# Retention in pairs of units ahead of two feed-forward layers

## The chip, the cores and the metric

The kernel runs on one core of a Trainium2 chip. The metric is the device time of one launch in microseconds (us), the median of three runs. TensorE is called PE here, VectorE DVE, ScalarE ACT, GpSimd POOL, and SyncE SP. SP only issues DMAs, in the order of its queue.

## The reference

The input is q, k and v for 4 batches, 8 heads, 576 positions and 64 features a head. Retention is attention without a softmax: the scores are weighted by a power of the distance, cut off above the diagonal, and multiplied with v. Two feed-forward layers of 2304 tokens, 512 features and 2048 hidden features follow.

```python
scores = scale * np.matmul(q, k.transpose(0, 1, 3, 2))
Dmat = np.where(rel >= 0, gamma[:, None, None] ** rel[None, :, :], 0.0)
attn = np.matmul(scores * Dmat[None], v)          # -> x [2304, 512]
h = x @ w_in;  x = (h * np.tanh(softplus(h))) @ w_out      # layer 1 (Mish)
h = x @ w2_in; out = (h * sigmoid(1.702 * h)) @ w2_out     # layer 2
```

All of it is in float32.

## The kernel before

Retention is cut into 20 units: per batch four chunks of 128 positions and a short one of 64 (`UNITS`, numbered 0 to 19; 4, 9, 14 and 19 are short, and 0, 5, 10 and 15 open a batch). One DMA of 1 MB brings a full unit into one of six buffers, a smaller one a short unit. The weighting is carried in the data: POOL scales v of a unit ahead of its use (`decay_v`, L870), and the last step scales the product (`gt`).

A unit has four groups of matmuls on PE. *Scores* (`sc`, L884) multiply k and q in 64-row halves of the array, 128 columns wide. *Carried* products (L940) multiply the state of the positions before with q, in 64 x 64 quarters. *Sums* (`ds`, L908) add k times v to the state, with 128 rows and 64 columns; ACT copies the sums to SBUF as the next `state` (`take`). *Masked* products (L952) multiply v with the masked scores `pm`, in the same shape as the sums. A unit that opens a batch has no carried group, a short unit has no sums. DVE makes `pm` out of the scores (L889) and `X` out of the finished products `o` (`finish`, L971). The scores of all units go round three PSUM banks, 7, 4 and 6.

`manual_schedule` keeps each engine's instructions as the code issues them. Up to unit 3 a unit is done after the other. From unit 4 on the scores of unit u + 1 stand ahead of the carried products, sums and masked products of unit u.

Layer 1 needs its weights as two float32r parts, a high one and a low one. `convert` makes them from 64-bit words, in steps that are dealt out over the units and, later, over the slots of layer 1: clamp (DVE), two copies to other words (ACT, `raw`), sign and shift (DVE), join (POOL, L220), high part (ACT, `w`), low part (L253, on POOL for the first two blocks of 128 hidden features, on DVE for the rest). `EARLY_AT` says at which unit the first two blocks are loaded and clamped; every later step waits for the next `position` call of its engine. A slot of layer 1 is one product `up` of a block of tokens with a block of weights (two slots per weight block: 512 tokens, then 256), one product `down` that belongs to three slots before, and `elementwise`: Mish and high part of `g` on ACT, low part of `g` on DVE (L460). Slots 0 and 1 stand between the last units: `up(0)` behind unit 17, `up(1)` behind unit 18, their `elementwise` behind the products of units 18 and 19. Slots 2 and on are in `first_layer`; slot 4 is the first that needs weight block 2.

Of the kernel before, what the change touches and what calls it, by code (L numbers as in the profile page):

```python
# [9 lines left out]
F32 = mybir.dt.float32  # L10
# [5 lines left out]
ALU = mybir.AluOpType  # L16
# [3 lines left out]
B, H, S, D = 4, 8, 576, 64  # L20
NT, DM, DFF = 2304, 512, 2048
P = 128
NPAIR = H // 2
NK = DM // P
# [77 lines left out]
def retention_mish_gelu_kernel(ctx: ExitStack, tc: tile.TileContext, qkv, w1, w2, first_unit, rests, out):  # L102
# [73 lines left out]
    def place(m):  # L176
        return keep if m in KEPT else late[0]
# [620 lines left out]

    def attention():
        with tc.tile_pool(name="att", bufs=1) as ap, tc.tile_pool(name="outs", bufs=1, space=PSUM) as outs:  # L800
            sc_banks = itertools.cycle((7, 4, 6))

            loaded = {}

# [46 lines left out]
            gt = ap.tile([P, NCH, NPAIR, P], F32, name="gt")  # L851
            load(0)
            unused = outs.tile([P, 2, NB], F32, tag="o1", name="unused")[:, 0, :P]
# [22 lines left out]

            def scores(u):
                n = CH[UNITS[u][1]][1]
                qt, kt = loaded[u][:2]
                sc = [quarters(psum(next(sc_banks), "sc")) for _ in range(2)]  # L880
                for p in range(NPAIR):
                    for j in range(2):
                        sl = slice(64 * j, 64 * j + 64)
                        nc.tensor.matmul(sc[j][rows(j, n), p, :n], lhsT=kt[sl, p, :], rhs=qt[sl, p, :], start=True, stop=True)  # L884
                pm[u] = []
                for j in range(2):
                    t = ap.tile([P, NPAIR, P], F32, tag="pm", name="pm", bufs=4)
                    at = rows(j, n)
                    nc.vector.tensor_tensor(  # L889
                        out=t[at, :, :n],  # L890
                        in0=sc[j][at, :, :n],
                        in1=cm[at, at].unsqueeze(1).to_broadcast([n, NPAIR, n]),
                        op=ALU.mult,
                    )
                    pm[u].append(t)

            def update(u):
# [23 lines left out]
                act(state[u % 2], sums[0][:, :, :D])  # L921
                return state[u % 2]

            def outputs(u, before, between=lambda: None):
                c = UNITS[u][1]
                n = CH[c][1]
                qt, _, v, _ = loaded[u]
                o = outs.tile([P, 2, NB], F32, tag=f"o{u % 2}", name="o")
                o = o[:, :, : 2 * P].rearrange("p r (c n) -> p r c n", c=2)

                def place(h):

                    j = h % 2
                    return o[64 * j : 64 * j + 64, h // 4, h // 2 % 2, :n]

                for p in (0, 2) if c else ():
                    for r in range(2):
                        for q in (p, p + 1):
                            sl = slice(64 * r, 64 * r + 64)
                            nc.tensor.matmul(  # L940
                                place(4 * r + q),
                                lhsT=before[sl, q, :],
                                rhs=qt[sl, q, :],
                                start=(p == 0),
                                stop=True,
                                skip_group_check=True,
                            )
                between()
                for h in range(H) if n == P else (0, 1, 4, 5, 2, 3, 6, 7):
                    r, p = divmod(h, NPAIR)  # L950
                    at, q = rows(r, n), h if n == P else p
                    nc.tensor.matmul(  # L952
                        place(h),
                        lhsT=v[at, q * D : (q + 1) * D],
                        rhs=pm[u][r][at, p, :n],
                        start=(c == 0 and p < 2),
                        stop=True,
                        skip_group_check=True,
                    )
                loaded.pop(u)  # L960
                return o

            def finish(u, o):
                b, c = UNITS[u]
                t0, n = CH[c]
                g0 = b * S + t0
                part = 0
                halves = lambda t: t.rearrange("p (r c) n -> p r c n", r=2)
                while part < n:
                    w = min(n - part, 2 * TH - (g0 + part) % (2 * TH))  # L970
                    nc.vector.tensor_tensor(  # L971
                        out=halves(cut(slice(None), g0 + part, w)),
                        in0=o[:, :, :, part : part + w],
                        in1=halves(gt[:, c, :, part : part + w]),
                        op=ALU.mult,
                    )
                    part += w

            decay_v(0)
            scores(0)  # L980
            act(gt[:, 0, :, : GROW[0]], first)
            for j, w in enumerate(GROW):
                for p in range(NPAIR):
                    act(gt[:, 0, p, w : 2 * w], gt[:, 0, p, :w], scale=grow[:, p, j : j + 1])
            for u in range(n_u):
                step = u - n_u
                if u - 1 in wide and wide.index(u - 1) + len(buffers) < len(wide):
                    n = wide[wide.index(u - 1) + len(buffers)]
                    load(n)
                    if n + 1 not in wide:  # L990
                        load(n + 1)
                if u + 1 < n_u:
                    decay_v(u + 1)
                position("pool", step)
                position("fetch", step)
                if u == 0:
                    for n in wide[NCH : len(buffers)]:
                        load(n)
                if NCH - 1 < u < n_u - 1:
                    scores(u + 1)  # L1000
                position("act early", step)
                x_jobs = [split_x((0, SIDE)[k // NK], k % NK) for k, at in enumerate(X_UNITS) if at == u]
                before = now[0]

                def step_state():
                    update(u)
                    now[0] = take(u)
                    if u == NCH - 1:
                        scores(u + 1)

                o = outputs(u, before, step_state)
                position("vector", step)
                for job in x_jobs:
                    job()
                if 0 < u < NCH - 1:
                    scores(u + 1)
                if u < NCH - 1:
                    n = CH[u + 1][1]
                    for p in range(NPAIR):
                        act(gt[:, u + 1, p, :n], gt[:, 0, p, :n], scale=steps[:, p, u + 1 : u + 2])  # L1020
                if u == n_u - 2:
                    elementwise(0, jobs=False)
                finish(u, o)
                if u == n_u - 1:
                    elementwise(1, jobs=False)
                if u == 0:
                    scores(1)
                position("act late", step)
                if u == n_u - 3:
                    up(0)  # L1030
                if u == n_u - 2:
                    up(1)

    first_ring = {}
    R_RING = [(tag, 2) for tag in ("w0a", "w0b", "x0", "x1")]
# [270 lines left out]
```

## Time and profile before

| | |
|---|---|
| median of 3 runs | 802.55 us (802.33 to 802.9) |
| profiled execution: time, span | 802.39 us, 800.7 us |
| PE busy | 795.6 us (99% of the span) |
| DVE, ACT, POOL busy | 564.0, 433.9, 200.6 us |
| retention on PE (first scores to `up(2)`) | 5.02 to 65.28 us |
| layer 1, first slot with weight block 2 | 72.40 us |

The span goes from the first to the last recorded instruction; the time lies 1.69 us above it. PE is busy from end to end, so a time is read best from the chain of waits, which gives the moments at which one group of matmuls follows another; a group that takes longer than its like has a wait in it. The other engines matter where one of their instructions is what PE waits for.

### The profile page before, as it was taken

To read this page: it belongs to the slowest core of one execution; us is meant where nothing else is said; L and a number is where in the kernel's file an instruction comes from. 1 tells how busy PE (TensorE), PEld (TensorE's weight loads), DVE (VectorE), ACT (ScalarE), POOL (GpSimd) and SP (SyncE) were. 2 spreads that over 40 slices of the span, in tenths; PEclk is the share of its full clock that TensorE was granted. 3 is DMA by queue.
4 is the path that set the end of the run, shared out by engine and by line. 5 is a ranking of instruction groups with operands and counts; after the bars stand their busy time and mean duration, and the time that the engine had idled before them with its cause. 6 is when DMAs were issued, how large, how long until landed. Compare 5 with 4: busy or idle time off the path is not lost.

```text
span 800.7 us, 14255 instructions
## 1 busy us (share of the span) xinstructions
PE 795.6 (99%) x5394; PEld 754.1 (94%) x5394; DVE 564.0 (70%) x980; ACT 433.9 (54%) x845; POOL 200.6 (25%) x262
## 2 busy tenths in 40 slices
PE   9999999999999999999999999999999999999998
PEld 8888888889999999999999999999999999999998
DVE  4788888877676766577667376898555887656775
ACT  4247676756665655666566464664233763234542
POOL 3684222210576640367560051000000000000000
PEclk9999999999999999999999999999999999999999
DMA  9985768845889995698996599888878888888884
GB/s 365 417 357 186 261 212 276 288 144 211 281 294 343 311 312 167 215 328 301 335 312 214 202 349 379 262 275 269 295 256 248 256 275 285 277 251 255 251 272 159
DMA packets 92325, 219.15 MB, mean 274 GB/s; under 512 B 6496, under 2 KB 52576, under 8 KB 90464
## 3 DMA queue, kind: packets, MB, share of 16 engines
q1 hardware_dynamic: 92112, 218.04, 80.8%
q8 instruction: 43, 0.70, 0.3%
q14 instruction: 26, 0.21, 0.1%
q10 hardware_dynamic: 144, 0.20, 0.1%
HBM read 169.45 MB, written 48.76 MB: 273 GB/s over the span
## 4 chain that ended last, share of the span: by engine, by line
PE 98%; DVE 1%; ACT 0%; issue 0%; DVEq 0%
PE p L734 22%; PE p L685 21%; PE acc L1107 17%; PE p L1170 15%; PE h L419 8%; PE acc L440 8%; PE sc L884 3%; PE o L952 2%; PE ds L908 1%; PE o L940 1%; PE unused L856 1%; DVE cs L478 0%; DVE u L478 0%; DVE X L144 0%; ACT cs L135 0%; DVE cy L355 0%
## 5 line engine op out<-in xcount | busy, mean ns | idle before, releaser
L685 PE MATMUL p<-xop,ring 128*128 128x384 f32 x1008 | 175.6, 334 | 0.4 <-DVE cs L478 0.4
L685 PEld LDWEIGHTS p<-xop,ring 128*128 128x128 f32 x1008 | 174.7, 188 | 0.8 <-DVE cs L478 0.7
L734 PE MATMUL p<-g,ring 128*128 128x384 f32 x1008 | 175.2, 334 | 0.0
L734 PEld LDWEIGHTS p<-g,ring 128*128 128x128 f32 x1008 | 174.8, 188 | 0.0
L1107 PE MATMUL acc<-g,w 128*128 128x512 f32 (+1 forms) x768 | 143.8, 337 | 0.0
L1107 PEld LDWEIGHTS acc<-g,w 128*128 128x128 f32 x768 | 124.3, 188 | 17.1 <-DVE g L478 0.3
L1170 PE MATMUL p<-xop,ring 128*128 128x384 f32 x672 | 128.4, 337 | 0.0
L1170 PEld LDWEIGHTS p<-xop,ring 128*128 128x128 f32 x672 | 115.8, 188 | 0.3
L135 ACT ACTIVATE g<-cs 128x384 fp32r<-128x384 f32 x168 | 79.0, 517 | 60.3 <-PE p L734 60.0
L478 DVE TENSOR_TENSOR g<-cs,g 128x384 fp32r<-128x384 f32 x168 | 90.0, 554 | 26.7 <-ACT g L135 25.0
L135 ACT ACTIVATE cs<-cs 128x384 f32<-128x384 f32 x72 | 37.8, 526 | 104.6 <-DVE cs L478 104.6
L478 DVE TENSOR_TENSOR g<-c,g 128x384 fp32r<-128x384 f32 x64 | 44.5, 695 | 39.7 <-ACT g L135 39.3
L440 PE MATMUL acc<-g,w 128*128 128x512 f32 (+1 forms) x384 | 72.3, 337 | 0.0
L440 PEld LDWEIGHTS acc<-g,w 128*128 128x128 f32 x384 | 60.2, 190 | 7.6
L135 ACT ACTIVATE c<-p 128x384 f32<-128x384 f32 x64 | 31.3, 489 | 53.9 <-PE p L1170 53.7
L220 POOL TENSOR_TENSOR raw<-raw 128x512 int32<-128x512 int32 x32 | 36.4, 1138 | 79.5 <-DVE raw L216 71.8
L345 POOL TENSOR_TENSOR cy<-cy 128x128 f32<-128x128 f32 x88 | 54.9, 634 | 5.2
L478 DVE TENSOR_TENSOR cs<-cs 128x384 f32<-128x384 f32 x96 | 53.4, 556 | 0.8
L220 POOL TENSOR_TENSOR cy<-cr 128x256 int32<-128x256 int32 x38 | 31.5, 848 | 63.4 <-DVE cr L216 58.9
L419 PE MATMUL h<-x,w 128*128 128x512 f32 x192 | 46.4, 390 | 0.0
L478 DVE TENSOR_TENSOR c<-p,c 128x384 f32<-128x384 f32 x48 | 26.5, 553 | 24.2 <-ACT c L135 13.1
L419 PEld LDWEIGHTS h<-x,w 128*128 128x128 f32 x192 | 35.9, 188 | 7.7 <-DVE pm L889 0.3
(94 smaller groups left out, 958.4 us busy)
## 6 DMA issues: line engine op xcount, KB each, us to landing
ring<-stream SPq DMA_DIRECT2D x168, 512.0 KB, 4.6
ring<-first_stream SPq DMA_DIRECT2D x56, 512.0 KB, 5.0
stream<-cy SPq DMA_DIRECT2D x22, 896.0 KB, 5.0
raw<-w_dram SPq DMA_DIRECT2D x32, 512.0 KB, 7.7
unit<-qkv_dram SPq DMA_DIRECT2D x14, 1024.0 KB, 12.5
cr<-w_dram SPq DMA_DIRECT2D x19, 512.0 KB, 5.6
stream<-X SPq DMA_DIRECT2D x10, 896.0 KB, 5.4
first_stream<-cy SPq DMA_DIRECT2D x16, 512.0 KB, 3.0
```

Source lines behind the costliest of these rows:

```text
L135: nc.scalar.activation(out=o, in_=i, func=f, scale=scale, bias=bias)
L220: nc.gpsimd.tensor_tensor(out=o, in0=upper, in1=bits, op=ALU.add)
L345: nc.gpsimd.tensor_tensor(out=v[:, o], in0=v[:, a], in1=v[:, b], op=op)
L419: nc.tensor.matmul(h[:, :n], lhsT=W[0, m // 2][:, m % 2, a, k * P : (k + 1) * P], rhs=xs[t, k][:, b, :n], start=((k, a, b) == order[0]), s ...
L440: nc.tensor.matmul(acc[t, e][:, :n], lhsT=W[1, m // 2][:, m % 2, a, e * P : (e + 1) * P], rhs=g[:, b, :n],  start=(begins(i) and a == 0 an ...
L478: eng.tensor_tensor(out=o, in0=a, in1=b, op=op)
L685: nc.tensor.matmul(banks[p], lhsT=w[:, k, a * P : (a + 1) * P], rhs=x[:, b, k], start=(p not in SAME and k == 0 and a == 0 and b == 0), st ...
L734: nc.tensor.matmul(banks[e, p], lhsT=w[:, e, a * P : (a + 1) * P], rhs=g[:, b], start=(p != 2 and r == 0 and a == 0 and b == 0), stop=(r = ...
L884: nc.tensor.matmul(sc[j][rows(j, n), p, :n], lhsT=kt[sl, p, :], rhs=qt[sl, p, :], start=True, stop=True)
L952: nc.tensor.matmul(place(h), lhsT=v[at, q * D : (q + 1) * D], rhs=pm[u][r][at, p, :n], start=(c == 0 and p < 2), stop=True, skip_group_che ...
L1107: nc.tensor.matmul(acc[t, e][:, :w], lhsT=W[1, m // 2][:, m % 2, a, e * P : (e + 1) * P], rhs=g[:, b, o : o + w], start=(m == 0 and a == 0 ...
L1170: nc.tensor.matmul(bank, lhsT=w[:, a, k * P : (k + 1) * P], rhs=x[:, b, k], start=(p in (1, 2, 7) and k == 0 and a == 0 and b == 0), stop= ...
```

## The change

From unit 7 on units go in pairs (7 and 8, 10 and 11, 12 and 13, 15 and 16, 17 and 18), by the new `cycle`. In a pair PE does the scores of both, those of the short unit if one follows, the carried products of the first, sums and masked products of the first and then of the second, the carried products of the second, and then carried and masked products of the short unit. Units 0 to 3, 5 and 6 go one at a time. The products of a pair go to one tile `o` of two banks, of which there is now one instead of two; the scores go round four banks, the fourth being `s`. The short unit's scores lie in one bank `x` (two before), and its products go to banks 6 and `s`. `finish` turns a whole pair into `X` at once. A unit's buffer is loaded anew behind its cycle. `up(0)`, `up(1)` and their `elementwise` stand behind unit 19.

At the start of a cycle `scale_to` issues the scaling of v for all its units and, if a short one is among them, for the unit after it too. `EARLY_AT` now loads the two first weight blocks at units 5 and 12 and clamps them at 10 and 17.

```diff
-EARLY_AT = ((2, 10), (9, 15))
+EARLY_AT = ((5, 10), (12, 17))
-            sc_banks = itertools.cycle((7, 4, 6))
+            spare_bank = lambda name: outs.tile([P, NB], F32, tag="s", name=name)
+            sc_banks = itertools.cycle(
+                [lambda: psum(7, "sc"), lambda: psum(4, "sc"), lambda: psum(6, "sc"), lambda: spare_bank("sc")]
+            )
-                sc = [quarters(psum(next(sc_banks), "sc")) for _ in range(2)]
+                if n == P:
+                    sc = [quarters(next(sc_banks)()) for _ in range(2)]
+                else:
+                    sc = [quarters(outs.tile([P, NB], F32, tag="x", name="sc"))] * 2
...
-                o = outs.tile([P, 2, NB], F32, tag=f"o{u % 2}", name="o")
+                if n < P:
+                    o = [quarters(psum(6, "o")), quarters(spare_bank("o"))]
+                else:
+                    o = outs.tile([P, 2, NB], F32, tag="o", name="o").rearrange("p r (c n) -> p r c n", c=2)
...
+            def cycle(units):
+                last = UNITS[units[-1]][1] == NCH - 2
+                tail = units[-1] + 1
+                scale_to(tail + last)
+                for i, u in enumerate(units):
+                    if u:
+                        scores(u)
+                    if i == 0:
+                        x_jobs = ahead(u)
+                if last:
+                    scores(tail)
+                place, o = places(units)
+                if 0 < UNITS[units[0]][1]:
+                    carried(units[0], place)
+                for i, u in enumerate(units):
+                    if i:
+                        x_jobs = ahead(u)
+                    update(u)
+                    take(u)
+                    masked(u, place)
+                    if i:
+                        carried(u, place)
+                    behind(u, x_jobs)
...
+                finish(units, o)
+                if last:
+                    x_jobs = ahead(tail)
+                    place, o = places([tail])
+                    carried(tail, place)
+                    masked(tail, place)
+                    behind(tail, x_jobs)
+                    finish([tail], o)
...
-                if u == n_u - 3:
-                    up(0)
-                if u == n_u - 2:
-                    up(1)
+            up(0)
+            up(1)
+            elementwise(0, jobs=False)
+            elementwise(1, jobs=False)
```

`ahead(u)` calls `position` for "pool", "fetch" and "act early" of that unit and issues its `split_x` copies; `behind(u)` calls it for "vector" and "act late".

On PE, units 12, 13 and 14 before, from the scores of unit 13 on (`rest` is a short unit's data, `unit_78` unit 15, the other `unit` rows units 12 and 13):

```order
L884 MATMUL sc<-unit 128x128 x8
L940 MATMUL o<-unit,state_76 64x128 x8
L908 MATMUL ds<-unit 64x64 x8
L952 MATMUL o<-pm,unit 64x128 x8
L884 MATMUL sc<-rest 64x64 x8
L940 MATMUL o<-unit,state_75 64x128 x8
L908 MATMUL ds<-unit 64x64 x8
L952 MATMUL o<-pm,unit 64x128 x8
L884 MATMUL sc<-unit_78 128x128 x8
L940 MATMUL o<-rest,state_76 64x64 x8
L952 MATMUL o<-pm,rest 64x64 x8
```

The same three units on PE now, from the scores of both on:

```order
L894 MATMUL sc<-unit 128x128 x16
L894 MATMUL sc<-rest 64x64 x8
L960 MATMUL o<-unit,state_76 64x128 x8
L919 MATMUL ds<-unit 64x64 x8
L971 MATMUL o<-pm,unit 64x128 x8
L919 MATMUL ds<-unit 64x64 x8
L971 MATMUL o<-pm,unit 64x128 x8
L960 MATMUL o<-unit,state_75 64x128 x8
L960 MATMUL o<-rest,state_76 64x64 x8
L971 MATMUL o<-pm,rest 64x64 x8
```

Groups of one shape now stand together, and the carried products of unit 14 follow the carried ones of unit 13 at once.

On POOL, around the joins of weight block 0 before (`unit`, `rest` and `unit_78` at L870 are the scaling of units 11 to 13, 14 and 15):

```order
L870 TENSOR_TENSOR unit<-unit,unit_78 128x512 x3
L220 TENSOR_TENSOR raw<-raw 128x512
L870 TENSOR_TENSOR rest<-rest,unit_78 128x256
L220 TENSOR_TENSOR raw<-raw 128x512
L253 TENSOR_TENSOR w_703<-raw,w_703 128x512
L870 TENSOR_TENSOR unit_78<-unit_78 128x512
L253 TENSOR_TENSOR w_749<-raw,w_749 128x512
L406 TENSOR_TENSOR side<-X,side 128x256
L870 TENSOR_TENSOR unit_79<-unit_79,unit_78 128x512
```

The same on POOL now:

```order
L877 TENSOR_TENSOR unit<-unit,unit_78 128x512 x3
L877 TENSOR_TENSOR rest<-rest,unit_78 128x256
L877 TENSOR_TENSOR unit_78<-unit_78 128x512
L220 TENSOR_TENSOR raw<-raw 128x512 x2
L253 TENSOR_TENSOR w_712<-raw,w_712 128x512
L253 TENSOR_TENSOR w_741<-raw,w_741 128x512
L406 TENSOR_TENSOR side<-X,side 128x256
L877 TENSOR_TENSOR unit_79<-unit_79,unit_78 128x512
```

The scaling of unit 15 has moved ahead of both joins, and that of unit 16 (`unit_79`) stays behind joins, low parts and one `side`.

On DVE, slots 1 to 3 of layer 1 before (L460 is the low part of `g` of slots 2 and 3, L253 the low parts of weight block 2, for `up` in `w_1057` and for `down` in `w_1089`):

```order
L204 TENSOR_SCALAR raw<-raw 128x512 x2
L460 TENSOR_TENSOR g<-h,g 128x512
L253 TENSOR_TENSOR w_1057<-raw,w_1057 128x512
L144 SCALAR_TENSOR_TENSOR raw<-raw 128x512
L216 TENSOR_SCALAR raw<-raw 128x512
L144 SCALAR_TENSOR_TENSOR raw<-raw 128x512
L216 TENSOR_SCALAR raw<-raw 128x512
L204 TENSOR_SCALAR raw<-raw 128x512
L460 TENSOR_TENSOR g<-h,g 128x256
L253 TENSOR_TENSOR w_1089<-raw,w_1089 128x512
```

The same slots on DVE now (block 2 is in `w_1076` and `w_1078`):

```order
L204 TENSOR_SCALAR raw<-raw 128x512 x2
L460 TENSOR_TENSOR g<-h,g 128x512
L144 SCALAR_TENSOR_TENSOR raw<-raw 128x512
L216 TENSOR_SCALAR raw<-raw 128x512
L144 SCALAR_TENSOR_TENSOR raw<-raw 128x512
L216 TENSOR_SCALAR raw<-raw 128x512
L204 TENSOR_SCALAR raw<-raw 128x512
L460 TENSOR_TENSOR g<-h,g 128x256
L253 TENSOR_TENSOR w_1076<-raw,w_1076 128x512
L253 TENSOR_TENSOR w_1078<-raw,w_1078 128x512
```

The low part that `up(4)` reads has moved from behind the low `g` of slot 2 to behind that of slot 3. On ACT, likewise, both high parts of block 2 (`w`) now stand between the `raw` copies of slot 2 and the Mish of slot 3, where one of them stood.

## Rows read from the trace of the kernel before

**Rows 1.** The page, busy time, share and instructions of each engine.

```profile
PE 795.6 (99%) x5394; PEld 754.1 (94%) x5394; DVE 564.0 (70%) x980; ACT 433.9 (54%) x845; POOL 200.6 (25%) x262
```

**Rows 2.** A stretch of retention: sum, busy of each engine, clock, DMA share, GB/s.

```profile
33.00:46.50 13.50, 13.46 (x290) 11.56 (x289) 12.02 (x21) 5.01 (x10) 6.66 (x8) 1.00 1.01 418
```

**Rows 3.** The chain of waits, 0 to 120 us: start, length, what.

```profile
19.47 1.42 PE sc L884 x16
...
21.29 1.39 PE sc L884 x16
...
24.16 1.09 PE sc L884 x16
25.26 0.60 PE o L940 x16
25.85 0.62 PE ds L908 x16
26.47 0.88 PE o L952 x16
...
46.57 1.09 PE sc L884 x16
...
63.02 1.63 PE h L419 x12
...
65.28 4.38 PE h L419 x24
...
72.40 2.72 PE h L419 x12
```

**Rows 4.** Timeline of the weight loads, 24 to 28 us: start, length, [idle before].

```profile
24.09 0.97 PEld L884 LDWEIGHTS sc<-unit 64*128 64x128 f32 x16 [0.17 <-issue]
...
26.24 0.86 PEld L952 LDWEIGHTS o<-pm,unit 128*64 128x64 f32 x16
```

**Rows 5.** Timeline of all engines in unit 0, 7 to 9.3 us.

```profile
7.83 1.26 PE L952 MATMUL o<-pm,unit 128*64 128x128 f32 x16 [0.24 <-DVE pm L889]
...
9.20 0.69 DVE L971 TENSOR_TENSOR X<-o,gt 128x512 f32<-128x512 f32 x1 [0.83 <-PE o L952]
```

**Rows 6.** Unit 15's load: its issue on SP, and its landing time.

```profile
30.60 2.87 SPq L829 DMA_DIRECT2D unit<-qkv_dram  x2
...
unit<-qkv_dram SPq DMA_DIRECT2D x1, 1024.0 KB, 12.1
```

**Rows 7.** Timeline of POOL: start, length, what.

```profile
44.71 1.04 POOL L220 TENSOR_TENSOR raw<-raw 128x512 int32<-128x512 int32 x1 [1.47 <-DVE raw L216]
45.71 1.30 POOL L253 TENSOR_TENSOR w<-raw,w 128x512 fp32r<-128x512 f32 x1
46.97 1.04 POOL L870 TENSOR_TENSOR unit<-unit 128x512 f32<-128x512 f32 x1
...
49.23 0.73 POOL L406 TENSOR_TENSOR side<-X,side 128x256 fp32r<-128x256 f32 x1
...
53.49 1.51 POOL L870 TENSOR_TENSOR unit<-unit,unit 128x512 f32<-128x512 f32 x1
```

**Rows 8.** Timeline of ACT: a `take`, and slots 2 and 3.

```profile
43.26 0.39 ACT L135 ACTIVATE state<-ds 128x256 f32<-128x256 f32 x1 [0.73 <-PE ds L908]
...
68.59 0.57 ACT L135 ACTIVATE h<-h 128x512 f32<-128x512 f32 x1
...
69.68 2.35 ACT L135 ACTIVATE raw<-raw 128x512 int32<-128x512 uint32 x4
71.93 0.68 ACT L135 ACTIVATE w<-raw 128x512 fp32r<-128x512 f32 x1
72.48 0.40 ACT L135 ACTIVATE h<-h 128x256 f32<-128x256 f32 x1
72.91 0.39 ACT L135 ACTIVATE g<-h 128x256 fp32r<-128x256 f32 x1
```

**Rows 9.** Timeline of DVE: the low part of weight block 2 for `up`.

```profile
71.00 0.68 DVE L253 TENSOR_TENSOR w<-raw,w 128x512 fp32r<-128x512 f32 x1
```

More of the change, by code (lines that the diff above doesn't have):

```diff
@@ L850, in attention @@
             )
-            gt = ap.tile([P, NCH, NPAIR, P], F32, name="gt")
+            cm_rest = ap.tile([P, REST], F32, name="cm_rest")
+            for r in range(2):
+                sl = slice(REST * r, REST * r + REST)
+                nc.vector.tensor_copy(out=cm_rest[sl], in_=cm[sl, sl])
+            gt = ap.tile([P, NPAIR, S], F32, name="gt")
             load(0)
-            unused = outs.tile([P, 2, NB], F32, tag="o1", name="unused")[:, 0, :P]
+            unused = outs.tile([P, 2, NB], F32, tag="o", name="unused")[:, 0, :P]
             zeros = nc.const_aps.tensor(0.0, (P, P), F32)
@@ L922, in take, with places, place @@
                 return state[u % 2]
[L924 to L927, printed above, removed]
-                o = outs.tile([P, 2, NB], F32, tag=f"o{u % 2}", name="o")
[L929 to L948, printed above, removed]
+            def places(units):
+                n = CH[UNITS[units[0]][1]][1]
+                if n < P:
+                    o = [quarters(psum(6, "o")), quarters(spare_bank("o"))]
+                else:
+                    o = outs.tile([P, 2, NB], F32, tag="o", name="o").rearrange("p r (c n) -> p r c n", c=2)
+                begun = set()
+                def place(u, h):
+                    r, j, i = h // NPAIR, h % 2, units.index(u)
+                    sl, p = slice(64 * j, 64 * j + 64), h // 2 % 2
+                    first_one = (r, j) not in begun
+                    begun.add((r, j))
+                    return (o[r][sl, p, :n] if n < P else o[sl, r, p, P * i : P * i + P]), first_one
+                return place, o
@@ new lines, in carried, with masked @@
+            def carried(u, place):
+                qt = loaded[u][0]
+                before = state[(u - 1) % 2]
+                for h in (0, 1, 4, 5, 2, 3, 6, 7):
+                    r, p = divmod(h, NPAIR)
+                    sl = slice(64 * r, 64 * r + 64)
+                    o, first_one = place(u, h)
+                    nc.tensor.matmul(
+                        o, lhsT=before[sl, p, :], rhs=qt[sl, p, :], start=first_one, stop=True, skip_group_check=True
+                    )
+            def masked(u, place):
+                n = CH[UNITS[u][1]][1]
+                v = loaded[u][2]
@@ L959, in outputs, with finish @@
                     )
[L960 to L965, printed above, removed]
+            def finish(units, o):
+                b, c = UNITS[units[0]]
+                t0, n = CH[c][0], sum(CH[UNITS[u][1]][1] for u in units)
                 g0 = b * S + t0
@@ new lines, in finish @@
+                    if n < P:
+                        for r in range(2):
+                            sl = slice(2 * r, 2 * r + 2)
+                            i = o[r][:, :2, part : part + w]
+                            nc.vector.tensor_tensor(out=x[:, sl], in0=i, in1=g[:, sl], op=ALU.mult)
+                    else:
+                        i = o[:, :, :, part : part + w]
+                        nc.vector.tensor_tensor(out=halves(x), in0=i, in1=halves(g), op=ALU.mult)
+                    part += w
@@ new lines, in attention, with scale_to, ahead, behind @@
+            scaled = [0]
+            def scale_to(u):
+                while scaled[0] < min(u + 1, n_u):
+                    decay_v(scaled[0])
+                    scaled[0] += 1
+            def ahead(u):
+                position("pool", u - n_u)
+                position("fetch", u - n_u)
+                position("act early", u - n_u)
+                return [split_x((0, SIDE)[k // NK], k % NK) for k, at in enumerate(X_UNITS) if at == u]
+            def behind(u, x_jobs):
+                position("vector", u - n_u)
+                for job in x_jobs:
+                    job()
+                position("act late", u - n_u)
@@ new lines, in cycle @@
+            def cycle(units):
+                last = UNITS[units[-1]][1] == NCH - 2
+                tail = units[-1] + 1
+                scale_to(tail + last)
+                x_jobs = []
+                for i, u in enumerate(units):
[17 more added lines that the diff above has]
+                    behind(u, x_jobs)
+                if units[0] < NCH - 1:
+                    c = units[0] + 1
+                    t0, n = CH[c]
+                    for p in range(NPAIR):
+                        act(gt[:, p, t0 : t0 + n], gt[:, p, :n], scale=steps[:, p, c : c + 1])
+                finish(units, o)
[6 more added lines that the diff above has]
+                    finish([tail], o)
+                for u in units:
+                    loaded.pop(u)
+                    w = wide.index(u) + len(buffers)
+                    if w < len(wide):
+                        load(wide[w])
+                        if wide[w] + 1 not in wide:
+                            load(wide[w] + 1)
@@ L980, in attention @@
+            scale_to(0)
             scores(0)
-            act(gt[:, 0, :, : GROW[0]], first)
+            act(gt[:, :, : GROW[0]], first)
             for j, w in enumerate(GROW):
                 for p in range(NPAIR):
[L984 to L1020, printed above, removed]
-                if u == n_u - 2:
[L1022 to L1028, printed above, removed]
-                if u == n_u - 3:
-                    up(0)
-                if u == n_u - 2:
-                    up(1)
```

37 lines of the change are left out of this document (21 added, 16 removed).

## The prediction

> **What bounds the kernel now.** The busy times come first: PE works 99% of the span, so only what PE no longer does, or no longer waits for, can shorten the time [rows 1]. The stretches of retention come second. [...] The chain of waits comes third, and it gives a unit on PE: 1.09 us of scores, 0.60 of carried products, 0.62 of sums and 0.88 of masked ones, 3.19 together [rows 3]. Then the timelines of POOL, ACT and DVE, for the places where the new order makes PE wait for them.
>
> **Gain on PE: changes of shape.** Behind the sums the masked products of the same array shape start without a gap; ahead of scores, which are of another, the weight loads idle 0.17 us [rows 4]. What a change costs follows from the groups: the masked group, which has no change ahead of it, takes 0.88 us. Scores have as many columns, two matmuls at a time too, and should take 0.88; carried products run four at a time (0.44), sums have half the columns (0.44). Sum 2.64 of 3.19, and 0.55 left for three changes, 0.18 each. I count the changes in the two orders, from the end of unit 3 to `up(2)`: 41 before, 25 now (12 per batch of pairs before, 7 now; five times in and out of layer 1's shape before, once now). Sixteen fewer at 0.18 are 2.9 us less; at the visible idle of 0.17 they are 2.7, at the 0.21 of the scores (1.09 less 0.88) 3.4.
>
> **Gain: waits for banks.** Two groups of scores of units 5 and 6 take 1.42 and 1.39 us instead of 1.09 [rows 3]. The new order starts the next scores of each bank a unit later: 0.6 us less.
>
> **Loss at unit 5.** It opens a batch alone, so only its sums stand between its scores and its masked products. Unit 0 had that order already: its masked products took 1.26 us and waited 0.24 for `pm` before [rows 5], so about 0.6 us more than 0.88. Unit 6 has carried products too, as units 1 to 3 have, and these show no wait.
>
> **Loss at unit 11.** Its scores go to banks 6 and `s`, which hold the products of unit 9. `finish` of the pair (twice 0.69 [rows 5]) runs on DVE ahead of `finish` of unit 9, and ends some 0.3 us behind the moment at which PE is ready. Between 0 and 0.7 (one whole `finish` late); I take 0.3.
>
> These four give 2.9 + 0.6 - 0.6 - 0.3 = 2.6 us, and `up(2)` at 62.7 instead of 65.28. Two chains in the order of other engines take that back.
>
> **First chain: unit 14's carried products.** They need the state after unit 13. On ACT its copy stands behind the high part of weight block 0, this waits for the join on POOL, and the join now stands behind the scaling of unit 15, which waits for that unit's DMA. The DMA engines are full, and the same bytes are ahead of unit 15 in SP's queue, so it lands as before: 30.60 + 12.1 = 42.7 [rows 6]. Then scaling 1.0 and join 1.1 [rows 7], a high part of which ACT is free again after 0.55 (71.93 to 72.48), the copy 0.39 [rows 8], and 0.1 for the handovers: 45.9. Before, PE has done all that stands ahead of them at 46.57, where it turns to the scores of unit 15 first [rows 3]; nine of the sixteen changes lie ahead of that (1.6), so by the terms above PE is there at 46.57 - 1.6 - 0.6 + 0.6 + 0.3 = 45.3. So it waits 0.6, and whatever it gained until here beyond that is lost: the scores of unit 15 start at 45.9 + 0.6 = 46.5. The scores of 15 and 16, 2.0, and sums and masked products of 15, 1.5, bring it to 50.0. The sums of unit 16 need its scaling, which POOL does behind two joins, two low parts, and one `side`: 43.7 + 2 x 1.1 + 2 x 1.27 + 0.7 + 1.0 = 50.2 [rows 7]. With 0.5, 0.9 and 0.6 for the rest of the pair, unit 17 starts at 52.2. The last pair with its short unit takes 2 x 2.64 + 0.9 (half the columns) + four changes 0.7 = 6.9, `up(0)` 2.8 (2.72 as in slot 4, and 0.1), `up(1)` 1.44 (1.63 less the change behind it [rows 3]): `up(2)` starts at 63.4. The two waits, 0.6 and 0.2, put on 62.7 give 63.5, near enough. 1.9 us of the gain are left.
>
> **Second chain: `up(4)`.** Before, nothing held ACT up behind `up(1)`: its Mish came while units 18 and 19 were on PE. Now it starts at 63.4, and ACT has in its queue, one behind the other: Mish and high `g` of slot 1 (0.43 + 0.28), four `raw` copies (2.25, from 69.68 to 71.93), a high part (0.55), Mish and high `g` of slot 2 (1.09, from 68.59 to 69.68), four `raw` copies (2.25), two high parts (1.1), Mish and high `g` of slot 3 (0.43 + 0.39) [rows 8]. That is 8.8 us: 72.2. Behind it DVE makes the low `g` of slot 3 (0.4) and only then the low part of block 2 for `up(4)` (0.68 [rows 9]): 73.3. The third matmul of `up(4)` reads it. PE has 2.72 + 1.44 + 2.75 of `up(2)`, `up(3)` and `down(0)` in that time and would be at this matmul at 63.4 + 6.9 + 0.45 = 70.8. It waits 2.6 us. Before, the same matmul came at 72.40 + 0.45 = 72.85 [rows 3], and the low part was there at 71.68 [rows 9]. So `up(4)` is 0.5 us later than before, at the least nothing later if POOL and ACT hand over faster than I count.
>
> POOL's and DVE's instructions are often longer than their least (a scaling took 1.51 instead of 1.04 [rows 7]); I add 0.1. From block 3 on the steps stand in the same slots as before, two slots ahead of their use, so nothing more is won or lost: the sum is 0.6 us on the profiled 802.39, which lies 0.16 below the median, so 803.1 for a median.
>
> [...]
>
> **Rivals.** *The gain stays.* If the chain on ACT doesn't bind (its copies overlap more than in rows 8, or `up(4)` isn't held by the low part), the 1.9 us at `up(2)` reach the end: 800.6; with the first chain hidden too 799.9. For it speaks that PE alone sets every step of the chain now; against it that ACT's 8.8 us are a strict queue of which each piece is a row. Chance 0.17.
>
> *Slower: POOL's queue decides.* Six instructions stand on POOL between the landing of unit 15 and the sums of unit 16. At 0.25 us more each (half of what the row of 1.51 shows) unit 17 starts 1.5 us later, and everything behind it: 804.6; at 0.47 each, 805.9. It decides as soon as unit 16's scaling ends behind 50.0, and above 0.2 each it costs more than a measurement can miss. For it speaks the row of 1.51, against it that the others are at 1.04 and 1.30. Chance 0.20.
>
> *Slower: the clock.* [...] Chance 0.05.
>
> **How the numbers follow.** My forecast, both chains as worked out, has 0.58; its own range is 802.0 (each handover 0.1 faster, changes at 0.21) to 804.3 (0.2 more per POOL instruction). The measurement can't tell less than 0.2%, 1.6 us, from no change: faster is below 800.95, slower above 804.15. Faster gets nearly all of the first rival and little else, 0.16; slower the two others and a little of the forecast's upper end, 0.26; no change 0.58. The range that leaves out 2 in 10 reaches down to 800.5 and up to 805.3.
>
> **What would show it.** In the chain, scores of a pair of 2.0 us without a gap and sums and masked products of both at 2.8; a wait of PE ahead of unit 14's carried products (released by ACT) and of unit 16's sums (by POOL); `up(2)` near 63.4; in slot 4 a wait of some 2.6 us released by DVE's L253. If `up(4)` starts without a wait, the second chain is wrong; if unit 15's scores start well ahead of 46.5, the first. A granted clock below 1.00 around 73 us would show the last rival.

## The result, and the profile after

The changed kernel takes 811.86 us (810.9 to 812.82, four runs) against 802.66 us (802.33 to 802.9, four runs): a ratio of 1.0115 with a 95% interval of 1.0097 to 1.0132. It is slower, by 9.2 us, and the forecast of 803.1 us with its range up to 805.3 was wrong. The profiled execution took 810.9 us with a span of 809.2 us, 8.5 us above the span before. The two slower of the four runs (812.82 and 812.4 us) had a mean clock of 0.995 and 0.996, the two faster 0.998.

The page's busy times, which answer to [rows 1]:

```profile
PE 795.3 (98%) x5394; PEld 753.9 (93%) x5394; DVE 562.7 (70%) x978; ACT 434.1 (54%) x845; POOL 199.8 (25%) x262
```

The stretch of retention of [rows 2] (sum, busy of PE, PEld, DVE, ACT and POOL, clock, DMA share, GB/s):

```profile
33.00:46.50 13.50, 12.36 (x286) 11.35 (x288) 10.71 (x19) 4.55 (x9) 6.27 (x7) 1.00 1.01 422
```

PE is busy for as long as before, so what is new is idle time. The equal sums hide two changes, though: the pairs have 1.8 us less to do (windows of 24.00 to `up(0)`, further down), and ten matmuls of `up(4)` take 1.9 us more. In the stretch PE is idle for 1.14 of 13.5 us, where it was busy throughout.

The chain of waits after the change, from unit 7 to the middle of slot 4 (start, length, what; "issue" is time in which PE waited for nothing that the profile shows):

```profile
28.69 0.22 PE o L960 x6
28.91 0.79 issue
29.70 0.45 PE o L960 x8
...
34.04 0.64 PE sc L894 x7
34.68 1.14 issue
35.82 1.71 PE sc L894 x25
...
46.84 0.70 PE o L960 x20
47.54 1.72 issue
49.27 0.39 PE o L960 x10
...
49.95 1.99 PE sc L894 x32
...
55.12 0.12 issue
...
62.84 4.40 PE h L419 x24
...
78.34 1.12 DVE w L253
79.46 0.04 issue
79.51 4.14 PE h L419 x10
```

Four pauses without a name, 3.77 us together, lie inside groups of matmuls whose other members ran: after eight of the sixteen carried products of unit 7 (the six of the row above and two just ahead of them), after seven of the scores of unit 10, after four of the carried products of unit 14, and, for 0.12 us, after two of those of unit 16. Then `up(4)`: its third matmul comes at 79.51, where it came at 72.85 before [rows 3], so 6.66 us late; and its last ten matmuls take 4.14 us, not the 2.27 that ten of twelve had in [rows 3]. That is 1.87 more, and with 6.66 it is the whole 8.5 us.

The 6.66 us split at `up(2)`. Its first matmul is at 67.06 (62.84 and the 4.22 of `up(0)` and `up(1)`), 1.8 us later than before; from there to the third matmul of `up(4)` it is 12.45 us instead of 7.57, 4.9 more. The windows around slot 4:

```profile
72.40:80.70 8.30, 3.96 (x15) 2.59 (x15) 8.20 (x13) 6.17 (x12) 5.04 (x4) 0.95 1.00 344
79.90:83.40 3.50, 3.50 (x10) 2.76 (x9) 1.52 (x4) 0.00 (x0) 1.10 (x1) 0.51 0.83 331
```

PE is idle for half of the first, DVE busy in nearly all of it, and behind it the granted clock is 0.51.

### The profile page after: what moved, and what is told of

Its sections match the earlier page's. It is cut to its first block, busy times and chain, and to the rows that moved or that the text cites. A ratio compares the mean times of both kernels' runs of the same rounds, so it can differ in the third digit from the quotient of the medians.

```text
span 809.2 us, 14252 instructions
## 1 busy us (share of the span) xinstructions
PE 795.3 (98%) x5394; PEld 753.9 (93%) x5394; DVE 562.7 (70%) x978; ACT 434.1 (54%) x845; POOL 199.8 (25%) x262
## 4 chain that ended last, share of the span: by engine, by line
PE 94%; DVE 2%; DMA 1%; issue 1%; ACT 0%; SPq 0%
PE p L734 22%; PE p L685 20%; PE acc L1158 17%; PE p L1221 15%; PE acc L440 8%; PE h L419 8%; PE sc L894 2%; PE o L971 2%; DMA unit<-qkv_dram 1%; PE o L960 1%; PE ds L919 1%; DVE raw L144 0%; DVE cs L478 0%; DVE raw L216 0%; DVE raw L204 0%
## 5 line engine op out<-in xcount | busy, mean ns | idle before, releaser
L478 DVE TENSOR_TENSOR cs<-cs 128x384 f32<-128x384 f32 x96 | 53.4, 556 | 0.8
L419 PE MATMUL h<-x,w 128*128 128x512 f32 x192 | 48.6, 402 | 4.3 <-DVE w L253 3.7
```

The source lines that it names most:

```text
L419: nc.tensor.matmul(h[:, :n], lhsT=W[0, m // 2][:, m % 2, a, k * P : (k + 1) * P], rhs=xs[t, k][:, b, :n], start=((k, a, b) == order[0]), s ...
L478: eng.tensor_tensor(out=o, in0=a, in1=b, op=op)
```

## The unnamed pauses of retention

The windows between the pauses give the number of matmuls and of weight loads in each (x):

```profile
28.91:34.68 5.77, 4.98 (x127) 4.38 (x127) 2.16 (x4) 1.28 (x3) 4.55 (x4) 1.00 1.02 415
34.68:47.54 12.86, 11.72 (x253) 10.66 (x253) 10.09 (x20) 4.55 (x9) 5.72 (x6) 1.00 1.01 423
47.54:55.12 7.58, 5.86 (x127) 5.25 (x127) 4.23 (x8) 2.72 (x7) 7.58 (x9) 1.00 1.01 411
```

127 + 127 = 254, 253 + 253 = 506 and again 254: but for a few missing records these are 256, 512 and 256 instructions. The page lists a DMA queue of the kind "instruction". The 5394 matmuls and as many weight loads of PE make 43 blocks of 256 (the last one not full), as many as this queue has packets (packets, MB, share of 16 engines):

```profile
q8 instruction: 43, 0.70, 0.3%
```

The DMA queues in the windows from 33.50 to 34.55 us and from 46.80 to 47.90 us, ahead of the ends of two of the pauses, hold one such packet each:

```profile
q1 hardware_dynamic: 58, 0.43, 100.7%
q8 instruction: 1, 0.02, 5.6%
...
q1 hardware_dynamic: 63, 0.42, 93.9%
q8 instruction: 1, 0.02, 5.6%
```

This suggests that PE's instructions come in blocks of 256, one packet of 16 KB (0.70 MB by 43) each, through the same DMA engines as the loads. PE entered a block at 29.70 and 35.82 (each the end of a pause); the packet with the next one began at 33.60 and 39.72, 3.9 us later, and the pause at 35.82 ended 2.2 us after its packet began. Counted on by 256 instructions, the five blocks that PE entered from 22.26 us on took 6.0 to 7.4 us each, at DMA shares of 1.00 to 1.03: 3.8 to 4.9 us until the next packet began, and at the four pauses 2.2 to 2.5 us from there until PE went on. In the old order PE needs 6.4 us for 256 instructions (3.19 us for a unit's 128, [rows 3]); the pairs are busy for 5.0 to 5.9 us per block in the windows above, and PE waits. Being faster may be only a part of it: by the same count, the next packet began 2.5 to 4.1 us after PE entered a block in the two traces of the old order with full loads (the kernel before and the run with layer 1 behind unit 19, below), so mostly sooner than now. Why it begins later in the new order is not shown.

That gives three theories to tell apart. **Supply:** PE's own instructions come too late, and that makes the pauses. **Conversion:** the late weight conversions hold `up(4)`, whatever retention does. **Clock:** the pause at `up(4)` costs another 1.9 us through the clock.

## The experiments

**Sixteen instructions more ahead of everything.** Four more of the matmuls with zeros at the start, two records of each kind per matmul.

```diff
-WARM = 9
+WARM = 13
```

> The changed kernel with 13 warm-up matmuls instead of 9, so 16 more PE instructions (weight loads and matmuls) ahead of everything. In the changed kernel PE stands still four times where the profile names no releaser: 0.8 us inside unit 7's carried products, 1.1 us after 7 records of unit 10's scores, 1.7 us after 4 records of unit 14's carried products, 0.1 us inside unit 11's carried products. These places are 256 PE instructions apart, or 512. Theory 'instruction supply': PE's own instructions come in blocks of 256 through the DMA engines and the next block is not there yet. Then every wait stands 16 instructions (8 matmul records) earlier in the program: at the end of unit 9's masked products instead of inside unit 10's scores, and inside unit 13's carried products instead of unit 14's. Rival 'a bank or an engine': each wait stays at the same matmul. The time is within 2 us of 811.9 by both.

One run took 812.66 us. The chain of waits and the windows between the pauses:

```profile
28.62 0.98 issue
...
33.93 0.23 PE o L971 x15
34.15 1.63 issue
```

```profile
28.62:34.15 5.53, 4.55 (x128) 4.07 (x127) 1.73 (x4) 1.28 (x3) 4.46 (x4) 1.00 1.00 404
34.15:48.23 14.08, 12.45 (x254) 11.11 (x253) 11.12 (x19) 4.55 (x9) 5.34 (x7) 1.00 1.01 420
```

The pauses moved with the count, not with the work (the expectation's "inside unit 11's" is unit 16's, as above): the first now stands ahead of unit 7's carried products, the second inside unit 9's masked products, 256 instructions apart as before. No bank, load or engine sits at a count of instructions. Supply is shown.

**Half the load.** From unit 7 on a load brings q and k alone, 512 KB instead of 1 MB; v and the second copy of k, which the sums use, are old data.

```diff
-                        e1 = e + 2 * DM if u == 1 else 4 * DM
+                        e1 = e + 2 * DM if u == 1 or wide.index(u) >= len(buffers) else 4 * DM
```

> The changed kernel, but the loads of units 7 to 18 bring only q and k (512 KB instead of 1 MB); v and the second k of these units are left as the unit before left them in the buffer. Order and count of all PE, DVE, ACT and POOL instructions stay. Theory 'instruction supply': with the DMA engines no longer full the blocks of instructions come in time, the four unnamed waits of PE (about 4 us) go, retention becomes as short as its matmuls, up(2) starts near 63.0 instead of 67.1. The wait in slot 4 stays, since it starts from up(1): 811.9 - 4 = 808. Rival 'a bank or an engine': the waits stay, the time stays within 1 us of 811.9. A third reading, that units' data were late, would also shorten the time, but the waits would be named as waits for the units' loads.

807.96 us, ratio 1.0065 (1.0048 to 1.0082). The pauses at units 10 and 14 are gone, the one at unit 7, up to which the loads are full, stays at 0.79 us; the chain now has

```profile
33.64 2.43 PE sc L894 x31
...
59.38 4.43 PE h L419 x24
```

From 33.00 to 46.50 us PE is busy throughout, at a DMA share of 0.70. Retention ends 3.5 us sooner, with the same instructions. The wait in slot 4 is unchanged (3.75 us), and the ten matmuls behind it take 4.63 us, in an execution with a mean clock of 0.995: two causes, one behind the other.

**The second block's clamp one unit earlier.**

```diff
-EARLY_AT = ((5, 10), (12, 17))
+EARLY_AT = ((5, 10), (12, 16))
```

> The changed kernel with weight block 1 clamped from unit 16 on instead of 17, which lets block 2 start one unit earlier too; nothing else. Theory 'late low part': the wait of 4.2 us in slot 4 comes from block 2's low part standing behind slot 3's low g. It now stands behind slot 2's low g, some 4 to 5 us earlier, so the wait in slot 4 goes, and with it the half clock behind it (1.9 us): 805 to 807. Rival 'ACT's queue': slot 4 waits because ACT and DVE have too much to do between up(1) and up(4) wherever the low part stands; then at most 2 us go: 810. The waits in retention stay, by all theories.

804.22 us (nine runs), ratio 1.0019 (1.001 to 1.0029): of the 9.2 us lost, 7.6 are back with one number. `up(2)` starts at 66.93 and slot 4 follows without a wait, at a granted clock of 1.00 from there to 90 us:

```profile
74.10 2.72 PE h L419 x12
```

The timeline of DVE around the low part that `up(4)` reads:

```profile
71.50 0.68 DVE L460 TENSOR_TENSOR g<-h,g 128x512 fp32r<-128x512 f32 x1
72.10 0.68 DVE L253 TENSOR_TENSOR w<-raw,w 128x512 fp32r<-128x512 f32 x1
```

It stands behind the low `g` of slot 2 again, as before the change [rows 9], not behind that of slot 3. In retention the pauses at units 7 and 10 stay (1.08 and 1.14 us); the one at unit 14 gave way to a chain through the conversion of weight block 0, which ends in

```profile
52.14 1.01 POOL unit L877
```

This scaling of unit 16 is what the sums of unit 16 wait for, 0.5 us. It is the place of the forecast's second rival, but not its price: that rival had POOL's instructions longer, and here POOL stood idle for 3.1 us until DVE's shift ahead of the second join was done.

**Matmuls in the gap of slot 4.** Sixteen matmuls into a bank that nobody reads, ahead of `up(4)`, so that PE isn't idle for long.

```diff
+            if i == 4:
+                fill = psum(5, "fill")
+                for k in range(16):
+                    nc.tensor.matmul(fill, lhsT=W[0, 0][:, 0, 0, :P], rhs=xs[0, 0][:, 0, :NB], start=True, stop=True)
```

> The changed kernel with 16 more matmuls of 512 columns ahead of up(4), which write a bank that nobody reads; they take 3.5 us of the 4.8 in which PE stands still there. Theory 'clock': the wait let the granted clock fall to half, which stretched ten matmuls of up(4) from 2.3 to 4.1 us. With the gap filled the clock stays at 1.00 and the time falls by 1.9 us: 810.0. Rival: the clock falls anyway, or the ten matmuls are slow for another reason: 811.9, or later by what the filling takes if it isn't hidden (up to 3.5).

811.1 us, ratio 1.0101 (1.0086 to 1.0116), an interval that overlaps with that of the change itself. In the profiled execution (809.37 us) the sixteen took 3.79 us, and a wait of 1.03 us was left. The third matmul of `up(4)` came as late as without them, at a granted clock of 1.00:

```profile
79.56 2.56 PE L419 MATMUL h<-x,w 128*128 128x512 f32 x10 [1.03 <-DVE w L253]
```

```profile
79.50:83.00 3.50, 3.44 (x19) 3.03 (x20) 1.97 (x4) 0.99 (x2) 1.10 (x1) 1.00 0.91 361
```

2.56 us instead of 4.14: the clock of 0.51 costs 1.6 to 1.9 us there. This execution had a mean clock of 1.000; the three other runs had 0.997 and 0.998 and took 811.09 to 811.46, so the filling kept the clock up in one of four runs; the median moved by 0.8. That the ten matmuls are slow at the clock of 0.51 is shown by this one run and the clock's own rows; a cure is not.

**Half loads in the order of before.**

```diff
-                        e1 = e + 2 * DM if u == 1 else 4 * DM
+                        e1 = e + 2 * DM if u == 1 or wide.index(u) >= len(buffers) else 4 * DM
```

> The kernel before, with the loads of units 7 to 18 cut to q and k (512 KB instead of 1 MB), as in the run of the changed kernel with half loads; v and the second k stay what the buffer held. Theory 'instruction supply': the order before is slower on PE (3.2 us a unit, some 6.3 us per 256 PE instructions) and hardly waited for its instructions, so little is to be had: its short waits at units 9 and 14 go, 0.3 to 0.9 us, 801.8 to 802.4, against 3.9 us in the changed kernel. Rival 'full DMA engines slow everything': the same 3 to 4 us as in the changed kernel, 799.

802.71 us, ratio 1.0001 (0.9991 to 1.001). Lighter loads alone are worth nothing that the medians show: the order of before has no pauses to lose. But they don't bring every block in time. The profiled execution, the second slowest of ten (803.75), has one such pause,

```profile
47.25 1.04 issue
```

at the same count of instructions as the changed kernel's pause at 47.54, and it ends 2.4 us after a packet began (45.89); the DMA share from 41.00 to 47.25 us was 0.96 there.

**Half loads and the earlier clamp together.**

> The changed kernel with both causes taken away: half loads from unit 7 on (v and the second k of these units aren't loaded) and weight block 1 clamped from unit 16 on. If the two causes are all that is wrong, both gains add: 811.9 - 3.9 - 7.6 = 800.4, up(2) near 63.5, no wait in slot 4, and what is left against the kernel before is the gain by fewer changes of the array's shape, about 2 us. Rival: with up(2) earlier, slot 4 waits again for ACT and DVE, since their queue starts at up(1) and the data of blocks 2 and 3 come no earlier; then 802 to 803.

801.51 us, ratio 0.9989 (0.998 to 0.9998), between what the two theories gave. With both causes largely out of the way the pairs are, by the medians, 1.2 us faster than the order of before with the same loads (802.71; single runs of the two overlap), less than half of the 2.6 us that I had for PE alone. A pause of 0.80 us at unit 7 is left (full loads up to there), and the scores of units 15 and 16 take 2.57 us instead of 2.06, as those of 16 wait for the `finish` of units 12 to 14. It leaves v's loads out, so it is no version to use.

**Layer 1 behind unit 19, in the order of before.** `up(0)`, `up(1)` and their `elementwise` move behind the loop over units; nothing else.

```diff
...
-                if u == n_u - 3:
-                    up(0)
-                if u == n_u - 2:
-                    up(1)
+            up(0)
+            up(1)
+            elementwise(0, jobs=False)
+            elementwise(1, jobs=False)
```

> The kernel before with one part of the change alone: up(0), up(1) and their elementwise steps behind unit 19, units in the old order, EARLY_AT as before. Theory 'block 2 was late because block 1 was moved': here block 2 keeps its place (its low part behind slot 2's low g), so no wait comes up in slot 4; four changes of shape fewer are worth 0.4 to 0.7 us: 801.9 to 802.6. Rival 'layer 1 behind the last unit is what starts ACT too late': a wait of 1 us or more in slot 4, 803.5 or more.

802.34 us, ratio 0.9998 (0.9989 to 1.0007). This part of the change costs nothing by itself, and slot 4 has no wait (`up(4)` at 72.36): that ACT starts on slot 1 only behind unit 19 does not by itself hold `up(4)`. It also gives the cleanest measure of the pairs, since the same 802 matmuls lie between 24.00 us and `up(0)`. The windows of that stretch, of this kernel (to 61.04) and of the changed one (to 62.84):

```profile
24.00:61.04 37.04, 36.83 (x802) 31.77 (x801) 31.27 (x53) 14.24 (x31) 26.91 (x27) 1.00 0.91 373
```

```profile
24.00:62.84 38.84, 35.07 (x802) 31.39 (x801) 26.08 (x47) 11.93 (x27) 23.28 (x25) 1.00 0.87 357
```

PE has 1.76 us less to do with the pairs, and waits 3.77 us instead of 0.21.

**Pairs only at the end.** Units 5 to 16 one at a time, 17 and 18 as a pair, and the earlier clamp.

```diff
-EARLY_AT = ((5, 10), (12, 17))
+EARLY_AT = ((5, 10), (12, 16))
...
-            single = NCH + 2
+            single = 17
```

> The changed kernel with only the last two units as a pair (17 and 18, then 19), all others one at a time, and weight block 1 clamped from unit 16 on. Theory 'instruction supply': units one at a time need a block of 256 PE instructions in 6.3 us, as before, and it comes in time; the last pair runs when the loads are done and keeps its gain (five changes of shape, 0.9 us, and 0.4 to 0.7 for layer 1 behind it): 801.3 to 802.0. Rival: one at a time, the units that open a batch wait for their masked scores (0.6 us at units 10 and 15), and unit 14 for the chain by POOL: 803 to 804.

805.39 us, ratio 1.0034 (1.0021 to 1.0047), above the ranges of both theories. The new code does a single unit's scores right ahead of its own products, where the order of before has them a unit ahead; the masked products then wait for `pm`, as the rival had it, and sums and masked products of units 5, 10 and 15 take 2.0 to 2.2 us instead of 1.5. Pauses of 1.21 and 0.38 us stay, and here the supply theory erred: units one at a time do not get their blocks in time either. Ahead of the longer one,

```profile
29.27 1.21 issue
```

the packet began at 28.11, 5.4 us after PE entered the block before. The run changed two things at once, and what each of them cost is open.

**The blocks loaded in units 2 and 9 again**, clamped at 10 and 16.

```diff
-EARLY_AT = ((5, 10), (12, 17))
+EARLY_AT = ((2, 10), (9, 16))
```

> The new order with layer 1's two early blocks loaded in units 2 and 9 as before, converted in 10 and 16 (as in the run with 16 alone, which took 804.2). Instruction supply sets retention's end: the waits of about 1 us inside unit 7's carried products, unit 10's scores and unit 14's carried products stay, up(0) does not come before 61.0 (where the old order with the ups behind has it), and the time is 802.3 to 804.2. Rival, conversion of block 1 on DVE and POOL sets it (its steps stood in the chain from 37 to 53 us in the run with 16 alone): loaded three units earlier its steps lie elsewhere, up(0) comes near 60.5 and the time is below 802.0.

804.74 us, ratio 1.0028 (1.0016 to 1.004). `up(0)` comes at 62.75, the pauses at units 7 and 10 stay (0.80 and 1.41 us), and the chain goes through DVE and POOL up to 53.4 as in the run with 16 alone. What differs is unit 14, where PE now waits for ACT's copy of unit 13's state:

```profile
48.38 0.36 ACT L135 ACTIVATE state<-ds 128x256 f32<-128x256 f32 x1
...
48.79 0.46 PE L960 MATMUL o<-rest,state 64*64 64x64 f32 x16 [1.34 <-ACT state L135]
```

That is the forecast's first chain: with the weight blocks loaded earlier unit 15's load lands later, POOL scales it at 45.28 instead of 42.69, and join, high part and copy follow. The time is that of the run with 16 alone (804.22; the intervals overlap), so the earlier loads win nothing, and the rival falls.

**The whole table of before** (2 and 10, 9 and 15), so that only the order of units differs.

```diff
-EARLY_AT = ((5, 10), (12, 17))
+EARLY_AT = ((2, 10), (9, 15))
```

> The new order with the table of before, blocks loaded in units 2 and 9, converted in 10 and 15: the order of units alone is changed. Instruction supply: the same waits, no wait in slot 4, clock at 1.00 throughout, 802.3 to 804.2. Rival, the table is needed by the pairs: a wait of PE for POOL's scaling of unit 15 or 16 behind the conversions, of 1 us or more, and 804.5 to 806.

805.79 us, ratio 1.0043 (1.0026 to 1.006), in the rival's range, though the wait that the rival names is not there: PE waits nowhere for POOL's scaling. It has the forecast's first chain, piece by piece: the timeline of POOL, ACT and PE,

```profile
45.24 1.04 POOL L877 TENSOR_TENSOR unit<-unit 128x512 f32<-128x512 f32 x1 [4.13 <-DMA unit<-qkv_dram]
...
46.25 1.04 POOL L220 TENSOR_TENSOR raw<-raw 128x512 int32<-128x512 int32 x1
...
47.31 0.69 ACT L135 ACTIVATE w<-raw 128x512 fp32r<-128x512 f32 x1 [1.37 <-POOL raw L220]
...
47.91 0.36 ACT L135 ACTIVATE state<-ds 128x256 f32<-128x256 f32 x1
...
48.32 0.19 PEld L960 LDWEIGHTS o<-rest,state 64*64 64x64 f32 x4 [0.30 <-ACT state L135]
```

where unit 15's load lands 2.5 us later than in the changed kernel, and a pause of 1.25 us follows behind the four matmuls. That pause ends 2.3 us after its packet began (47.63), so the 0.30 us of waiting ahead of it may have cost nothing. The order of units costs 3.3 us with the old table and 1.5 us with the best one tried; the clamp at 17 made it 9.2.

No version of the pairs with full loads was faster than the kernel before. That a lighter way to bring in the same bytes, or fewer instructions, would free the pairs' gain was not tried.

## Why the prediction was wrong

Against the forecast 3.7 us were lost up to `up(2)` (67.06 for 63.4), 2.5 more from there to the third matmul of `up(4)` (12.45 for the 9.9 between 63.4 and 73.3), and 1.9 in the slow matmuls behind it.

**Gain of shapes, 2.9 us: about right, but not collected.** The terms up to unit 19 gave 2.6 us, of which 0.7 was for the four changes around layer 1, so 1.9 for the units; the windows show 1.76. Scores of a pair take 1.99 us (forecast 2.0). The scores of units 10 and 11 took 2.43 us with half loads, 0.4 more (forecast 0.3, for `finish` of unit 9). Unit 5 took 0.8 more (forecast 0.6); a block ends within its masked products, so some of that may be a short pause. Of layer 1's 0.7, `up(0)` and `up(1)` show 0.4: 4.65 before, 1.63 of it in [rows 3], and 4.2 now.

**The step that failed first: "The DMA engines are full", taken for the data of the units alone.** The sum took each group's duration as all that PE needs. It left out what feeds PE itself: 3.77 us of pauses for instruction blocks. [Rows 2] had half of it, DMA engines at 1.01; I applied that to the units' data and not to PE's instructions, which by the packets above come through the same engines. Taken off by subtraction, the pauses would leave `up(0)` at 59.07, where the forecast had 63.4 less 4.24, 59.2. That these agree is luck: 0.8 us of the forecast's figure are the two waits of the first chain, which did not come.

**First chain: right in mechanism, did not bind.** The join ran at 43.69 and unit 13's copy at 46.08 (forecast 43.7 and 45.5), but PE, already late by two pauses, came at 46.84. Its second half was too small: unit 16's scaling ended at 52.19, not 50.2, since POOL stood idle for 2.24 us ahead of the second join until DVE's shift was done. PE came to the sums behind it at 53.42, a third pause later, so this did not show. With the blocks loaded in units 2 and 9 the chain does make PE wait, 1.34 and 0.30 us, as above.

**Second chain, the other step that failed: right place, wrong queue, too small.** The wait at `up(4)` is on DVE's L253, as forecast; 2.6 us were expected, and 3.74 measured, behind a start of `up(4)` that had itself waited 0.60 for ACT. ACT's queue had the right length: 9.0 us from `up(1)`'s last product (67.26) to the end of the high `g` of slot 3 (76.27), forecast 8.8. Behind it I had 1.1 us of DVE; it took 3.2, as DVE's timeline with POOL's join in it shows:

```profile
75.03 0.73 PE L419 MATMUL h<-x,w 128*128 128x512 f32 x2 [0.60 <-ACT w L135]
...
75.47 0.43 DVE L216 TENSOR_SCALAR raw<-raw 128x512 int32<-128x512 int32 x1
...
75.97 1.42 POOL L220 TENSOR_TENSOR raw<-raw 128x512 int32<-128x512 int32 x1 [1.09 <-DVE raw L216]
...
76.53 1.15 DVE L216 TENSOR_SCALAR raw<-raw 128x512 int32<-128x512 int32 x1
77.59 0.42 DVE L204 TENSOR_SCALAR raw<-raw 128x512 f32<-128x512 f32 x1
...
77.93 0.41 DVE L460 TENSOR_TENSOR g<-h,g 128x256 fp32r<-128x256 f32 x1
78.26 1.79 DVE L253 TENSOR_TENSOR w<-raw,w 128x512 fp32r<-128x512 f32 x2
...
79.51 0.91 PE L419 MATMUL h<-x,w 128*128 128x512 f32 x2 [3.74 <-DVE w L253]
```

DVE was not free when ACT was done: it had the second shift (L216) and a clamp (L204) of the conversion still ahead of the low `g` (L460), and the shift took 1.15 us beside POOL's join instead of 0.43. So the term that was too small is DVE's: 3.2 us for 1.1. The chain of waits lies on DVE alone from 69.19 us to the third matmul, so DVE's queue was the longer one. DVE's new order stood ahead of the forecast; I had added ACT's queue alone, as if DVE had nothing to do but to follow. Clamping weight block 1 one unit earlier takes the whole wait away (the run with 16). In the trace of the changed kernel the nine shifts of L216 that began within an operation of POOL took 0.57 to 1.15 us, and each ended 0.28 to 0.29 us behind that operation (this one at 77.68, POOL's join at 77.39); the 55 others took 0.43.

**The clock: given 0.05, and it came.** Ten matmuls of `up(4)` took 1.87 us more than ten of their like before, at a granted clock of 0.51 behind 3.74 us of waiting. The chance of 0.05 was my estimate, and no row of before shows the clock fall behind a gap of PE; the sum had made the gap 2.6 us. The clock was at 1.00 through retention with pauses of up to 1.72 us and, in one run, behind the filled gap of which 1.03 us were left; at which length of a gap it falls is not shown.

**Short scores in one bank: no delay.** The forecast had none for them. Where they ran without a pause, their weight loads took 0.54 us as before.

## What to carry to other kernels

Where the DMA share was 1.00 to 1.03 here, PE waited 3.77 us for its own instructions: in such a stretch count PE's matmuls and weight loads per microsecond before making them denser, and look for "issue" pauses a fixed number of instructions apart (256 or 512 here). When a chain passes from one strict queue to another, add up both queues, the second with all that it has to do by itself and with its durations beside POOL (a shift of up to 1.15 us instead of 0.43 here). One number in a table (17 or 16) was worth 7.6 us here: after a reordering, the steps that were dealt out for the old order must be placed anew and looked at first.

## What was not expected of the hardware

- By the counts, PE's instructions arrive in packets of 16 KB, 256 in each (43 packets, 0.70 MB, for twice 5394 instructions); with the DMA share at 1.00 to 1.03 a packet began 3.8 to 4.9 us after PE entered the block before, and at the four pauses PE went on 2.2 to 2.5 us after the packet began.
- The pauses ascribed to this, of 0.12 to 1.72 us, have no releaser in the profile and lay inside groups of like matmuls (the first after eight of the sixteen carried products of unit 7).
- A DVE shift of 128 x 512 that began within a POOL operation took 0.57 to 1.15 us, any other 0.43; in the kernel before too (1.15 at 73.38 us).
- Behind a wait of 3.74 us ten matmuls of `up(4)` ran at 0.41 us each, at a granted clock of 0.51, where 0.23 is their pace before [rows 3].
